# Query-weight casts moved from GpSimd to ScalarE, and a value copy moved ahead of the next unit's seed, in a two-layer linear-attention and gated-MLP kernel

## The chip, the cores and the metric

The kernel runs on one core of a Trainium2 chip. The metric is the device time of one execution in microseconds (us); the number given for a kernel is the median of several runs. One further execution is taken by the hardware profiler, and all rows of the profile come from it. The core's engines run side by side, each through its own instruction list in order: TensorE (PE in the profile, its weight loads PEld), VectorE (DVE), ScalarE (ACT), GpSimd (POOL), and SyncE (SP), which here issues the DMAs. [...]

## What is computed

Two kinds of blocks alternate, attention (A), MLP (B), A, B, each behind a layer norm and added to the running activations `x` (2048 x 1024, bf16). The changed code belongs to the second A.

```python
H = 32; Dh = D // H
qkv = (x @ wqkv) -> q, k, v per head
phi = lambda t: where(t > 0, t + 1, exp(t)) + 1e-6
pq, pk = phi(q), phi(k)
kv = einsum("bhsd,bhse->bhde", pk, v)      # summed over all tokens
z  = einsum("bhsd->bhd", pk)
num = einsum("bhqd,bhde->bhqe", pq, kv)
den = einsum("bhqd,bhd->bhq", pq, z)[..., None] + 1e-6
A   = (num / den) @ wo

B   = ((x @ w_gate) * (x @ w_up)) @ w_down

x = x + A(layernorm(x)); x = x + B(layernorm(x))    # twice
```

## The kernel before

**Stages.** Layers A, B, A, B follow one another in one program. Tokens are taken in 16 tiles of 128 and 4 groups of 512. The order of every engine's instructions is written out by hand: the program text, run once, appends each instruction to its engine's list, so what is written first runs first on that engine. Small plans (`at(step, f, ...)`) hang side work, such as layer norms, casts and loads, behind numbered steps of a stage's main loop.

**The stage of the change.** `kv_seven` makes keys and values of the second A layer. It computes each 2 x 2 block product with seven block products instead of eight, a Winograd form: sums of weight blocks (`w_sum`) and of activation blocks (`x_sum`) are made beforehand, and intermediate sums are taken out of PSUM between the products. The work comes in eight units (two per token group; each handles two token tiles). A unit has 14 steps, in the order of `SEQ`: `1k 5k 1v 6k 2k 6v 7k 5v 7v 4k 2v 3k 4v 3v`. The digit is the product, the letter says keys or values. Each step is four matmuls of 128x128 by 128x512 (L577) into one of five PSUM banks that the whole stage keeps: `ak`, `av` (products 1, 6, 7, 4), `ck`, `cv` (products 5, 3) and `b` (product 2, keys and values by turns).

Banks accumulate: 6k is added to what 1k left in `ak`, after that was read. So TensorE may begin a step only when earlier contents of its bank have been read. The readers of one unit, in the program's order:

- after 1k, ScalarE copies `ak` into `b`, the *seed* (L582), onto which 2k is then added;
- after 1v, 6v and 7v, ScalarE copies `av` to a temporary (L558); VectorE later adds `b` or `cv` to it and writes a value block (L561);
- after 6k and 7k, ScalarE copies `ak` into a 128x1024 scratch `wide` (L587); VectorE adds `ck` to its halves (L566), half 1 behind 7k and half 0 behind 3k;
- after 2k and 4k, ScalarE takes an exponential of the bank (L287, 128x512), and VectorE finishes phi (L291, L293) into the key scratch `pks`;
- after 3k, ScalarE takes the *wide* exponential over the 128x1024 scratch (also L287), and VectorE finishes it one step later;
- after 4v, ScalarE copies `av` to the last value block (`out4`, L569). `later(2, ...)` puts this two steps on: behind step 0 (1k) of the next unit, and there behind the seed.

The next unit's 1v (its step 2) overwrites `av`, so it needs that copy. After each unit but the first, 16 small matmuls (`kp`, L528) accumulate keys times values of the unit before.

**Side work in this stage.** Layer norms of the second half of the tokens: `ln_stats` on VectorE, then for some tiles `ln_norm` (two small ScalarE instructions, L258 and L260, then VectorE) and for the others `ln_rstd` (L242, L243) with `ln_apply` (L251, ScalarE, 128x1024), and then a DMA transpose (L274, SP). `x_sum` (L218) on VectorE. Loads and casts of the query weights: `load_w("q", 0)` and `load_w("q", 1)` behind steps 8 and 9 of unit 0 (1 MB each, SP's queue), then `cast_q` (L183) on GpSimd behind steps 20, 24, ... 48: eight casts of 128x1024 from bf16 to scaled f16, in place.

**Buffers.** `slots` is a first-in, first-out list of 17 scratch buffers; who calls `get()` first takes the one that was put back longest ago. `pks` and `wides` take theirs at the stage's start, before the query loads.

**Afterwards** `q_step` (L784) multiplies by the cast query weights: the first half (n = 0) for its steps 0 to 3, the second half for 4 to 7.

Of the kernel before, what the change touches and what calls it, by code (L numbers as in the profile page):

```python
# [9 lines left out]
ACT = mybir.ActivationFunctionType  # L10
ALU = mybir.AluOpType
# [24 lines left out]
def kernel(  # L36
# [11 lines left out]
    nc = tc.nc  # L48
# [4 lines left out]
    KD = D // P  # L53
# [5 lines left out]
    NB = 512  # L59
# [26 lines left out]
    def v3(s, n):  # L86
        return s[:].rearrange("p (k n) -> p k n", n=n)

    def h3(s, n):
        return s[:].bitcast(F16).rearrange("p (k n) -> p k n", n=n)  # L90
# [4 lines left out]
    def load_cols(view, n, parts=1):  # L95
        s = slots.get()
        w = KD // parts
        for r in range(parts):
            nc.sync.dma_start(out=v3(s, NB)[:, r * w:(r + 1) * w, :],
                              in_=view[:, r * w:(r + 1) * w, n * NB:(n + 1) * NB])  # L100
        return s
# [42 lines left out]
    for i in range(NV):  # L144
        vb = const.tile([P, KD, VW], BF16, tag=f"vb{i}", name=f"vb{i}")
# [10 lines left out]
    scw = const.tile([P, 6], F32, tag="scw", name="scw")  # L156
# [23 lines left out]

    def cast_q(n, i):
        s = wA["q"][n]
        nc.gpsimd.tensor_scalar(out=h3(s, NB)[:, 2 * i:2 * i + 2, :], in0=v3(s, NB)[:, 2 * i:2 * i + 2, :],  # L183
                                scalar1=scw[:, 4:5], scalar2=None, op0=ALU.mult)

    def w_blocks(which):
        a, b = (h3(s, NB) for s in wA[which])
# [19 lines left out]
    def x_blocks(g):  # L207
        x = h3(xnTs[(2, g)], NB)
        t = h3(xgs[g], 2 * P).rearrange("p (s k) n -> p s k n", k=KH)
        return x[:, 0:KH, 0:2 * P], x[:, KH:KD, 0:2 * P], x[:, 0:KH, 2 * P:NB], x[:, KH:KD, 2 * P:NB], t  # L210
# [73 lines left out]
    def phi_exp(b, c):  # L284
        m = temps.get()
        e = m[:].bitcast(BF16)[:, 0:b.shape[-1]]
        nc.scalar.activation(out=e, in_=b, func=ACT.Exp, bias=lns2[:, c:c + 1], scale=kaps[:, c:c + 1])  # L287
        return m, e
# [202 lines left out]
    def kv_seven(kvp):  # L491
        plan = {}

        def at(step, f, *args):
            plan.setdefault(step, []).append((f, args))

        for t, i in zip(range(2 * TPG, NT), (3, 8, 17, 31, 36, 45, 59, 64)):
            at(i, ln_stats, 2, t, (0,))
            if i % 14 == 8:
                at(i + 5, ln_norm, 2, t)  # L500
                at(i + 6, tr_tile, 2, t)
            else:
                at(i + 4, ln_rstd, 2, t)
                at(i + 6, ln_apply, 2, t)
                at(i + 7, tr_tile, 2, t)
        at(66, lambda: temps.put(st8.pop()))
        for g, i in ((1, 19), (2, 45), (3, 75)):
            for j in range(4):
                at(i + 2 * j, x_sum, g, j)
        at(8, load_w, "q", 0)  # L510
        at(9, load_w, "q", 1)
        for n in range(DC):
            for i in range(4):
                at(20 + 16 * n + 4 * i, cast_q, n, i)
        at(90, lambda: wA.update(o=[load_cols(wo_v, 0)]))

        pks = slots.get()
        pkv = v3(pks, D)
        SEQ = "1k 5k 1v 6k 2k 6v 7k 5v 7v 4k 2v 3k 4v 3v"
        bk = {key: banks.get() for key in ("ak", "av", "ck", "cv", "b")}  # L520
        wides = slots.get()
        wide = wides[:].bitcast(F32).rearrange("p (u n) -> p u n", n=D)

        def kp(t, first, last):
            u = t // TPG * 2 + t % 2
            r = 2 * (u % 2) + t % TPG // 2
            for c in range(KD):
                nc.tensor.matmul(out=kvp[c // 3][:, (c % 3) * VW:(c % 3) * VW + VW],  # L528
                                 lhsT=pkv[:, r, c * P:(c + 1) * P], rhs=vbs[r][:, c, :],
                                 start=first and c % 3 == 0, stop=last, skip_group_check=True)  # L530

        def tiles(u):
            return u // 2 * TPG + u % 2, u // 2 * TPG + u % 2 + 2

        def unit(u):
            g, pr = divmod(u, 2)
            b11, b21, b12, b22, t = x_blocks(g)
            lhs = {1: b11, 2: b21, 3: b22, 4: t[:, 3], 5: t[:, 0], 6: t[:, 1], 7: t[:, 2]}
            tm = {}
            r0 = 2 * (u % 2)  # L540

            def pk(i, n):
                return pkv[:, r0 + i, n * NB:(n + 1) * NB]

            def vb(i, n):
                return vbs[r0 + i][:, n * (NB // P):(n + 1) * (NB // P), 0:P]

            def w4(a):
                return a[:].rearrange("p (c f) -> p c f", f=P)

            wd2 = wide[:, u % 2]

            def later(n, f, *args):
                at(u * 14 + j + n, f, *args)

            def copy(key, b):
                tm[key] = temps.get()
                nc.scalar.copy(out=tm[key][:], in_=b[:])  # L558

            def add(out, key, b):  # L560
                nc.vector.tensor_tensor(out=out, in0=w4(tm[key]), in1=w4(b), op=ALU.add)  # L561
                temps.put(tm.pop(key))

            def addw(n, b):
                v = wd2[:, n * NB:(n + 1) * NB]
                nc.vector.tensor_tensor(out=v, in0=v, in1=b[:], op=ALU.add)  # L566

            def out4(b):
                nc.scalar.copy(out=vb(0, 1), in_=w4(b))  # L569

            for j, step in enumerate(SEQ.split()):
                i, w = int(step[0]), step[1]
                key = "b" if i == 2 else ("c" if i in (3, 5) else "a") + w
                b = bk[key]
                rhs = w_rhs(w, i)
                for k in range(KH):
                    nc.tensor.matmul(out=b[:], lhsT=lhs[i][:, k, pr * P:(pr + 1) * P], rhs=rhs[:, k, :],  # L577
                                     start=k == 0 and (i in (1, 5) or i == 2 and w == "v"), stop=k == KH - 1,
                                     skip_group_check=True)
                if i == 1:  # L580
                    if w == "k":
                        nc.scalar.copy(out=bk["b"][:], in_=b[:])  # L582
                    else:
                        copy("1v", b)
                elif i in (6, 7) and w == "k":
                    n = i - 6
                    nc.scalar.copy(out=wd2[:, n * NB:(n + 1) * NB], in_=b[:])  # L587
                    if i == 7:
                        later(1, addw, 1, bk["ck"])
                elif i == 6:  # L590
                    copy("6v", b)
                elif i == 7:
                    copy("7v", b)
                    add(vb(1, 1), "7v", bk["cv"])
                elif i == 3:
                    if w == "k":
                        addw(0, b)
                        later(1, phi_end, wd2, pkv[:, r0 + 1, :], 0, *phi_exp(wd2, 0))
                    else:
                        add(vb(1, 0), "6v", b)  # L600
                elif i == 2:
                    if w == "k":
                        phi_end(b[:], pk(0, 0), 0, *phi_exp(b[:], 0))
                    else:
                        add(vb(0, 0), "1v", b)
                elif i == 4:
                    if w == "k":
                        phi_end(b[:], pk(0, 1), 0, *phi_exp(b[:], 0))
                    else:
                        later(2, out4, b)  # L610
                for f, args in plan.pop(u * 14 + j, ()):
                    f(*args)

        for u in range(2 * NG):
            unit(u)
            if u > 0:
                for t in tiles(u - 1):
                    kp(t, u == 1 and t == 0, False)
            if u % 2 == 1:
                slots.put(xgs.pop(u // 2))  # L620

        for i in sorted(plan):
            for f, args in plan[i]:
                f(*args)
        slots.put(*wA.pop("k"), *wA.pop("v"), wS.pop("k"), wS.pop("v"), wS.pop("d"), wides)
        banks.put(*bk.values())
        wA["o"].append(load_cols(wo_v, 1))

        def rest():
            for t in tiles(2 * NG - 1):  # L630
                kp(t, False, t == NT - 1)
            slots.put(pks)
        return rest

    def load_w(which, n):
        wA.setdefault(which, []).append(load_cols(wqkv_v, {"q": 0, "k": DC, "v": 2 * DC}[which] + n))
# [645 lines left out]
```

## Time and profile before

| | us |
|---|---|
| runs of the kernel before (3) | 1502.18, 1501.54, 1501.65 |
| median | 1501.65 |
| the profiled execution's own time | 1502.76 |
| its span, first to last instruction | 1501.0 |
| units' matmuls (L577), from the first start to the last | 758.5 to 865.8 |
| busy in the window 800 to 814 (one unit): TensorE, VectorE, ScalarE | 13.70, 10.99, 8.79 |
| busy in the same window: GpSimd | 0.00 |
| the eight casts on GpSimd (L183), busy | 23.6 |

The rest of the span is layer B's products (L947, 3136 matmuls; L1187, 1568 matmuls) and the other parts of A. A row of the timeline reads: start, length, engine, line, operation, output and inputs, count of instructions merged into the row, and in brackets how long the engine was idle before it and what it had waited for. `b` is a PSUM bank, `s` a slot, `f` a temporary, `vb` a value block. Instructions of one engine overlap a little, so the next one's start can lie before the end of the one before. The mean granted TensorE clock of the profiled execution is 1.000 of full speed.

### The profile page before, as it was taken

The numbers are of one execution on the slowest core, as the hardware profiler recorded it, in microseconds if no ns is written. First come the engines' busy times: TensorE is split into PE (matmuls) and PEld (weight loads), VectorE is DVE, ScalarE is ACT, GpSimd is POOL, SyncE is SP. The second block draws the span as 40 slices with busy tenths as digits, with TensorE's granted clock in tenths as the row PEclk, the third lists the DMA queues.
The fourth block names the chain that finished last, engine by engine and source line by source line (L and its number), as shares of the span: only waits on it lengthen the run. The fifth ranks groups of instructions, "written<-read, shape, count | busy, mean of one in ns | idle before, by whom it ended". The sixth has DMA issues, their size and how long they took to land.

```text
span 1501.0 us, 18364 instructions
## 1 busy us (share of the span) xinstructions
PE 1488.1 (99%) x7075; PEld 683.3 (46%) x7109; DVE 988.4 (66%) x1659; ACT 803.9 (54%) x1177; POOL 114.1 (8%) x54
## 2 busy tenths in 40 slices
PE   9999999999999999999999999999999999999999
PEld 4454444444444444444444444444444444444444
DVE  6567989988676666667877586854445854444452
ACT  4678875776658477764546575623335223333420
POOL 0000004963000000000060000000000000000000
PEclk9999999999999999999999999999999999999999
DMA  8696136465479788759531101464333678343513
GB/s 245 172 304 232 57 92 202 132 208 153 130 211 313 250 263 263 246 200 267 164 84 23 42 29 28 132 235 168 121 125 109 188 261 325 113 168 113 209 61 130
DMA packets 219655, 253.90 MB, mean 169 GB/s; under 512 B 68528, under 2 KB 195504, under 8 KB 208816
## 3 DMA queue, kind: packets, MB, share of 16 engines
q1 hardware_dynamic: 219568, 252.74, 53.1%
q8 instruction: 55, 0.90, 0.2%
q14 instruction: 32, 0.26, 0.1%
HBM read 196.08 MB, written 40.89 MB: 158 GB/s over the span
## 4 chain that ended last, share of the span: by engine, by line
PE 96%; DVE 2%; ACT 1%; DMA 1%; issue 0%; SPq 0%; DVEq 0%; ACTq 0%
PE b L947 45%; PE b L1187 23%; PE b L784 7%; PE b L647 7%; PE b L815 7%; PE b L577 5%; PE b L798 1%; DMA s<-in_A_wqkv_dram 1%; PE b L666 1%; PE b L765 0%; PE b L528 0%; ACT b L582 0%; ACT vb L569 0%; DVE st L234 0%; DVE X L1160 0%
## 5 line engine op out<-in xcount | busy, mean ns | idle before, releaser
L947 PE MATMUL b<-s,s 128*128 128x512 f16 x3136 | 677.7, 379 | 0.0
L947 PEld LDWEIGHTS <-s 128*128 128x128 f16 x3136 | 306.8, 98 | 369.8
L1187 PE MATMUL b<-s,s 128*128 128x512 f16 x1568 | 339.1, 379 | 0.0
L963 DVE TENSOR_TENSOR f<-f,b 128x512 f32<-128x512 f32 x232 | 159.3, 687 | 223.7 <-ACT f L952 209.5
L952 ACT COPY f<-b 128x512 f32<-128x512 f32 x284 | 166.2, 585 | 224.8 <-PE b L947 224.8
L1187 PEld LDWEIGHTS <-s 128*128 128x128 f16 x1568 | 153.4, 98 | 185.0
L958 ACT COPY b<-b 128x512 f32<-128x512 f32 x104 | 59.3, 570 | 128.3 <-PE b L947 128.3
L444 ACT ACTIVATE s<-s,scw 128x1024 f16<-128x1024 bf16 x112 | 122.8, 1151 | 2.0 <-DMA s<-in_B_w_gate_dram 1.8
L784 PE MATMUL b<-s,s 128*128 128x512 bf16 (+1 forms) x508 | 119.9, 379 | 0.2
L815 PE MATMUL b<-s,s 128*128 128x512 bf16 x495 | 117.5, 379 | 1.1 <-DVE s L807 0.3
L913 ACT ACTIVATE s<-s,scw 128x1792 f16<-128x1792 bf16 x48 | 83.0, 1784 | 61.4 <-DMA s<-in_B_w_down_dram 61.4
L647 PE MATMUL b<-s,s 128*128 128x512 bf16 x500 | 111.3, 379 | 1.7 <-DMA s<-in_A_wqkv_dram 0.8
L868 POOL TENSOR_SCALAR s<-s,scw 128x1024 f16<-128x1024 bf16 x28 | 88.8, 3188 | 257.8 <-DVE X L817 244.1
L577 PE MATMUL b<-s,s 128*128 128x512 f16 x448 | 99.4, 379 | 3.6 <-ACT vb L569 3.5
L967 DVE SCALAR_TENSOR_TENSOR s<-f,b 128x512 f16<-128x512 f32 x108 | 74.2, 687 | 39.9 <-PE b L947 24.2
L967 DVE SCALAR_TENSOR_TENSOR s<-f,f 128x512 f16<-128x512 f32 x116 | 83.3, 718 | 4.5 <-DVE f L963 0.5
L815 PEld LDWEIGHTS <-s 128*128 128x128 bf16 x512 | 50.0, 98 | 60.9 <-DVE s L807 1.0
L647 PEld LDWEIGHTS <-s 128*128 128x128 bf16 x512 | 49.7, 98 | 60.7 <-issue 1.4
L784 PEld LDWEIGHTS <-s 128*128 128x128 bf16 (+1 forms) x512 | 50.0, 98 | 59.4
L234 DVE BATCH_NORM_STATS2 st<-X 128x6 f32<-128x512 bf16 x112 | 71.7, 681 | 2.6 <-DMA X<-in_A_x_dram 2.6
L577 PEld LDWEIGHTS <-s 128*128 128x128 f16 x448 | 43.5, 98 | 56.7 <-issue 6.4
L1095 DVE TENSOR_TENSOR s<-s,s 128x1024 f16<-128x1024 f16 x80 | 52.9, 678 | 23.4 <-PE b L1187 23.4
(123 smaller groups left out, 1113.2 us busy)
## 6 DMA issues: line engine op xcount, KB each, us to landing
s<-wc SPq DMA_DIRECT2D x56, 1024.0 KB, 6.6
s<-dc SPq DMA_DIRECT2D x32, 896.0 KB, 5.6
wc<-s SPq DMA_DIRECT2D x28, 1024.0 KB, 5.2
s<-in_B_w_down_dram SPq DMA_DIRECT2D x24, 896.0 KB, 5.6
s<-in_A_wqkv_dram SPq DMA_DIRECT2D x17, 1024.0 KB, 7.9
s<-in_B_w_down_dram SPq DMA_DIRECT2D x14, 1024.0 KB, 8.0
s<-in_B_w_gate_dram SPq DMA_DIRECT2D x28, 512.0 KB, 6.7
s<-in_B_w_up_dram SPq DMA_DIRECT2D x28, 512.0 KB, 7.7
```

Source lines behind the costliest of these rows:

```text
L444: nc.scalar.activation(out=h, in_=v, func=ACT.Copy, scale=scw[:, m:m + 1])
L577: nc.tensor.matmul(out=b[:], lhsT=lhs[i][:, k, pr * P:(pr + 1) * P], rhs=rhs[:, k, :], start=k == 0 and (i in (1, 5) or i == 2 and w == "v ...
L647: nc.tensor.matmul(out=b[:], lhsT=xnT[:, k, tl * P:(tl + 1) * P], rhs=w[:, k, :], start=(k == 0), stop=(k == KD - 1))
L784: nc.tensor.matmul(out=b[:], lhsT=w[:, k, j * P:(j + 1) * P], rhs=xnT[:, k, :], start=(k == 0), stop=(k == KD - 1))
L815: nc.tensor.matmul(out=b[:], lhsT=v3(pqs[g], G)[:, c, tl * P:(tl + 1) * P], rhs=v3(M[n], NB)[:, c, :], start=(c == 0), stop=(c == KD - 1))
L868: nc.gpsimd.tensor_scalar(out=h3(s, D)[:, i, :], in0=v3(s, D)[:, i, :], scalar1=scw[:, 2:3], scalar2=None, op0=ALU.mult)
L913: nc.scalar.activation(out=v.bitcast(F16)[:, r * w:(r + 1) * w], in_=v[:, r * w:(r + 1) * w], func=ACT.Copy, scale=scw[:, 2:3])
L947: nc.tensor.matmul(out=o[m][:], lhsT=W.get(j, m, st[i - 1], k), rhs=mv[i - 1][:, k, :], start=start and k == 0, stop=stop and k == KH - 1, ...
L952: nc.scalar.copy(out=d[m][:], in_=o[m][:])
L963: nc.vector.tensor_tensor(out=d[m][:], in0=d[m][:], in1=o[m][:], op=ALU.add)
L967: nc.vector.scalar_tensor_tensor(out=h3(hs[h], 2 * G)[:, pos, g * G:(g + 1) * G], in0=x[:], scalar=HS, in1=y[:], op0=ALU.mult, op1=ALU.mult)
L1187: nc.tensor.matmul(out=bank[(key, tl)][:], lhsT=lhs(i, j, tl), rhs=h3(wd[2 * pi + j // WPC], NB)[:, j % WPC, :], start=(j == 0 and i in (1 ...
```

## The change

Three edits in `kv_seven` and its helper. `cast_q` becomes a ScalarE activation (Copy with the same scale). The eight casts leave the plan: one is issued in each unit behind step 3k, ahead of the wide exponential, four for each half of the weights. The two loads of query weights leave the plan too and stand at the stage's head, before `pks` and `wides` take their slots. And `out4` is gone: the copy of the last value block is issued at step 4v itself.

```diff
     def cast_q(n, i):
         s = wA["q"][n]
-        nc.gpsimd.tensor_scalar(out=h3(s, NB)[:, 2 * i:2 * i + 2, :], in0=v3(s, NB)[:, 2 * i:2 * i + 2, :],
-                                scalar1=scw[:, 4:5], scalar2=None, op0=ALU.mult)
+        nc.scalar.activation(out=h3(s, NB)[:, 2 * i:2 * i + 2, :], in_=v3(s, NB)[:, 2 * i:2 * i + 2, :],
+                             func=ACT.Copy, scale=scw[:, 4:5])
...
-        at(8, load_w, "q", 0)
-        at(9, load_w, "q", 1)
         for n in range(DC):
-            for i in range(4):
-                at(20 + 16 * n + 4 * i, cast_q, n, i)
+            load_w("q", n)
         at(90, lambda: wA.update(o=[load_cols(wo_v, 0)]))
...
-            def out4(b):
-                nc.scalar.copy(out=vb(0, 1), in_=w4(b))
-
...
                 elif i == 3:
                     if w == "k":
                         addw(0, b)
+                        cast_q(*divmod(u, KD // 2))
                         later(1, phi_end, wd2, pkv[:, r0 + 1, :], 0, *phi_exp(wd2, 0))
...
                     if w == "k":
                         phi_end(b[:], pk(0, 1), 0, *phi_exp(b[:], 0))
                     else:
-                        later(2, out4, b)
+                        nc.scalar.copy(out=vb(0, 1), in_=w4(b))
```

## The prediction

> **What bounds the kernel now.** I read the page's busy line and chain of waits first, then the instructions of L577, the line that issues the changed stage's matmuls, and then the timeline over that stage.
>
> ```profile
> PE 1488.1 (99%) x7075; PEld 683.3 (46%) x7109; DVE 988.4 (66%) x1659; ACT 803.9 (54%) x1177; POOL 114.1 (8%) x54
> ...
> PE 96%; DVE 2%; ACT 1%; DMA 1%; issue 0%; SPq 0%; DVEq 0%; ACTq 0%
> ```
>
> TensorE is busy for 1488.1 of 1501.0 us, and 96% of the chain that ended last is its work. So only a hole in TensorE's stream can shorten the kernel. The instructions of L577 show who makes the holes of this stage:
>
> ```profile
> L577 PE MATMUL b<-s,s x448: 376/379/379, 758.5 to 865.8; 128*128 128x512 f16 x150
> its engine sat idle before it (us, times) until:
>   issue: 6.4, 10
>   ACT vb L569: 3.5, 7
> ```
>
> Seven times, once at each change from a unit to the next, TensorE waits for L569, ScalarE's copy of the value bank's last block. The "issue" row belongs to the weight loads: they idle between matmuls anyway. The timeline shows one change in full; this is unit 3 to unit 4 (units are counted from 0), and the other five late ones look alike:
>
> ```profile
> 801.70 10.52 PE L577 MATMUL b<-s,s 128*128 128x512 f16 x48 [0.30 <-ACT vb L569]
> ...
> 812.05 1.11 PE L528 MATMUL b<-vb,s 128*128 128x129 bf16 x16
> 812.58 1.24 ACT L287 ACTIVATE f<-s,lns,kaps 128x1024 bf16<-128x1024 f32 x1 [1.88 <-DVE s L566]
> ...
> 813.00 1.89 PE L577 MATMUL b<-s,s 128*128 128x512 f16 x8
> ...
> 814.06 0.57 ACT L582 COPY b<-b 128x512 f32<-128x512 f32 x1 [0.24 <-PE b L577]
> ...
> 814.54 0.59 ACT L569 CAST vb<-b 128x512 bf16<-128x512 f32 x1
> 815.19 10.52 PE L577 MATMUL b<-s,s 128*128 128x512 f16 x48 [0.30 <-ACT vb L569]
> ```
>
> ScalarE is free after the wide exponential, but its next instruction is the seed (L582), which needs the new unit's first product 1k; only behind that comes L569. TensorE does 1k and 5k (eight matmuls at 813.00), and then 1v must overwrite the bank that L569 still reads.
>
> The printed idle time is too small, because a matmul's modelled end (0.379 us) overlaps the next one's start. By starts: 48 matmuls run from 801.70 to 812.05, 10.35 us, 0.216 each. Eight from 813.00 would let the next start at 814.73; it starts at 815.19. **The hole is 0.46 us**, six times (restarts at 788.21, 801.70, 815.19, 828.68, 842.17 and 855.66, 13.49 apart): 2.78 us. The first change is worse:
>
> ```profile
> 768.95 1.10 DVE L291 TENSOR_SCALAR f<-f,scw,epss 128x512 bf16<-128x512 bf16 x1
> ...
> 771.28 0.68 DVE L566 TENSOR_TENSOR s<-s,b 128x512 f32<-128x512 f32 x1
> 772.00 1.24 ACT L287 ACTIVATE f<-s,lns,kaps 128x1024 bf16<-128x1024 f32 x1 [2.36 <-DVE s L566]
> 772.02 0.74 PEld L577 LDWEIGHTS <-s 128*128 128x128 f16 x4 [0.28 <-issue]
> ...
> 774.08 0.58 ACT L569 CAST vb<-b 128x512 bf16<-128x512 f32 x1
> 774.72 10.52 PE L577 MATMUL b<-s,s 128*128 128x512 f16 x48 [1.67 <-ACT vb L569]
> ```
>
> The 64 matmuls before it (timeline: 758.50, 14.54 us) end at 773.04 by the model, so the next could start 0.16 earlier (0.379 less 0.216), at 772.88. The hole to 774.72 is 1.84. Another 0.17 lies at 772.02: a weight load idles 0.12 in the steady stream (0.216 less its 0.098) and here 0.28. It starts 0.06 after L566 ended (771.96), which reads the bank that 5k overwrites. All holes together: 2.78 + 1.84 + 0.17 = 4.79 us.
>
> **The change, part by part.**
>
> *The value copy moves ahead of the seed.* No instruction is added; L569 now stands behind the wide exponential. At unit 3 to 4 the exponential starts at 812.58, and the next instruction on ScalarE can start 1.15 later (in another unit L258 starts at 799.98 after 798.83). The copy then runs 813.73 to 814.32, with its bank finished long before. 1v could start at 814.73: 0.35 to spare after the 0.06 of signalling (801.64 to 801.70 before). The other changes, likewise (exponential's start + 1.15 + 0.59 + 0.06 against 1k's start + 1.73): unit 1 to 2, 785.60 and 786.02, spare 0.35; 2 to 3, 798.83 and 799.50 (the restart at 801.70 less 0.46 and 1.73), spare 0.60; 4 to 5, 825.81 and 826.49, 0.61; 5 to 6, 839.57 and 839.98, 0.34; 6 to 7, 852.45 and 853.47, 0.95. All six holes close: 2.78.
>
> *The wait that this adds.* The seed now stands behind the copy. Late next would be 6k, which overwrites the bank that the seed reads, 0.86 (four matmuls) after 1v's start. At 3 to 4 the seed starts 0.48 behind the copy (the spacing of 814.06 and 814.54) and runs 814.21 to 814.78, 6k is due at 815.59. Tightest are units 2 and 4, where the norm's Ln and Exp (0.59 from L258's start to the seed's, 826.96 to 827.55) stand between copy and seed: at 4 to 5 the copy starts at 826.96, the Ln at 827.44, and the seed runs 828.03 to 828.60; 6k is due at 828.22 + 0.86 = 829.08, spare 0.4.
>
> *Eight casts on ScalarE.* The same form stands at L444, 128x1024 to f16 at 1.15 us, in the page. Eight make 9.2 us of ScalarE, each queued ahead of a wide exponential. They cost nothing if they fit ScalarE's idle time before that exponential, which waits for VectorE's L566: 2.36, 1.88, 1.61, 1.88, 1.61, 3.00, 2.40, 2.41 us for units 0 to 7 (timeline). In unit 0 this shrinks to about 1.67, by the next paragraph. All are above 1.15, the least spare 0.46. Without cover each would cost up to 1.15. Bounds of the cast: 1.13 (the shortest L444) and 1.23 (L251, as large, with two operands); I take 1.15, and nothing changes over that span.
>
> *Eight casts off GpSimd* (L183, 23.6 us from 760.32). Nobody waited for them. But in their time VectorE's L291 took 1.10 where the unit-3 row has 0.41, its wide form 1.46 against 0.55, and the wide L293 2.02 against 1.23. If the 0.69 at 768.95 is GpSimd's doing, L566 ends at 771.27 instead of 771.96. Then 5k's 0.17 closes, and the exponential starts at 771.31. The cast fits (L251 starts at 768.42, so the cast runs 769.55 to 770.70). The copy runs 772.46 to 773.05, and 1v starts at 773.11, where 772.72 was possible: gain 774.72 less 773.11, 1.61. If VectorE is no faster, the exponential stays at 772.00, the copy ends at 773.74 and 1v starts at 773.80: gain 0.92. I take 1.61: the three rows stretch only while GpSimd casts, though not always then (0.41 at 764.24). [...]
>
> *The query loads move to the stage's head.* They are two 1 MB transfers on SP's queue. The first transpose of the stage is issued behind step 10 of unit 0, they stood at steps 8 and 9, so they pass no other instruction of that queue. In the trace both are issued at 755.03 and used by 760.32; the median landing is 6.3 us. The first cast now wants its weights at 769.55. The loads take the two slots that the key scratch (pks) and the wide scratch had, and the other way round. Those scratches are first written at 762.56 (L587) and 764.68 (L293), after the last down-projection matmul (758.3). Cost nothing. The last cast ends near 864.7; the query matmuls begin at 866.96 with the other half of the weights.
>
> *Sum:* 2.78 + 1.61 = **4.4 us**, between 3.7 (0.92 at the first change) and 4.79 (every hole). The profiled execution took 1502.76 us, its span 1501.0 and 1.76 around it. That gives a span of 1496.6 and 1498.4 for such an execution. The median of the runs, 1501.65, lies 1.1 below the profiled one, so the forecast for it is 1497.3.
>
> **The rivals.**
>
> *The holes close by half.* The copy now depends on an exponential that waits for VectorE, with 0.35 us to spare in three changes; without holes, VectorE has 13.03 instead of 13.49 us for a unit. For it: VectorE is busy 11.0 of 14 us in the window from 800 to 814. Against: every unit shows VectorE idle before its wide exponential's result arrives (1.31 in most). If six holes keep 0.23 and the first gains 0.92: 2.3 us, 1499.3.
>
> *Saved here, waited for later.* If a later transfer or VectorE set the end, the 4.4 us would come back as a wait: 1501.6. Against: the next waits I see, 0.36 at 869.68 on VectorE and the output weights' second load (issued near 865.7, used at 877.5), follow TensorE's own progress and shift with it.
>
> *Slower: the query load blocks ScalarE.* GpSimd had nothing behind its casts; on ScalarE the first cast holds the exponential, the copy and the seed. The point is 770.15 (771.31 less 1.15): from there each microsecond of lateness stops TensorE as long. If the load were issued only with the transposes at 769.67 and took 7.9 (median landing of such loads over the kernel), the cast would run 777.6 to 778.7, the copy would end near 780.5, and 1v starts 5.8 later than before; less 2.8 for the six other holes that is 3.0 slower, 1504.6. Against: the load has a free queue and over 8 us of margin.
>
> **How the numbers follow.** Forecast 72%, half-closed 14%, no gain 8%, slower 6%. The likeliest gives 1497.3, its own range 1496.7 to 1498.0. To hold 8 in 10 I go to 1499.6, over the half-closed case, and down to 1496.6, all holes and 0.2 for the spread of the runs (0.6 us). A change of 0.2%, 3.0 us, is about what a measurement of this kernel can tell from none. The forecast lies beyond it, the half-closed case mostly within: faster 0.75, same 0.18, slower 0.07.
>
> **What would show it.** The profile after should have 1k, 5k and 1v in one stream at each change, so the group of L577 loses its 3.5 us behind the value copy; units 13.03 us apart; ScalarE in the order cast, wide exponential, copy, seed, with casts of 1.15 us; L291 at 0.41 in unit 0; no GpSimd work after the first down-projection casts; the query stage starting 4.4 us earlier. The prediction is wrong if the wide exponential starts later after 4k than now, if 6k waits for the seed, or if the first cast waits for a DMA.

## The result and the profile after

| | before | after |
|---|---|---|
| median of 13 runs, us | 1502.18 (1501.33 to 1502.66) | 1498.18 (1497.59 to 1499.31) |
| span of the profiled execution, us | 1501.0 | 1496.1 |
| units' matmuls, first to last start, us | 758.5 to 865.8: 107.3 | 758.0 to 860.9: 102.9 |
| GpSimd busy, us | 114.1 | 89.4 |
| ScalarE busy, us | 803.9 | 811.0 |

The changed kernel takes 0.9974 of the time before (95% interval 0.9966 to 0.9982): 4.0 us by the medians. The spans differ by 4.9, but 0.46 of that lies ahead of the stage, in code that is the same in both (its first matmul starts at 758.05 and before at 758.50). Over the ten traces of this case that start lies between 757.67 and 758.98, so it is a difference between executions. The stage itself is 4.4 us shorter.

The page's busy line and chain after:

```profile
PE 1489.2 (100%) x7109; PEld 683.0 (46%) x7109; DVE 985.5 (66%) x1659; ACT 811.0 (54%) x1185; POOL 89.4 (6%) x46
...
PE 97%; DVE 2%; DMA 1%; ACT 0%; SPq 0%; issue 0%; DVEq 0%; ACTq 0%
```

ScalarE's share of the chain, 1% before, is now printed as 0%. The units' matmuls are now issued by line L571:

```profile
L571 PE MATMUL b<-s,s x448: 376/379/380, 758.0 to 860.9; 128*128 128x512 f16 x150
its engine sat idle before it (us, times) until:
  issue: 1.2, 4
```

The seven waits for the value copy are gone; only the weight loads' "issue" row is left. It is worth reading: its four times are 0.27 and 0.37 in the first unit (at 759.06 and 761.04) and the 0.42 and 0.17 of the first change, shown below. The ten times of that row before were likewise the holes, as the weight loads see them: the timeline has 0.27 and 0.37 in the first unit, 0.28 and 1.95 at the first change and six of 0.58, together 6.4. The prediction took the row for an idling that is there anyway. The change from unit 3 to unit 4 in the timeline (L605 is the value copy, L576 the seed, L183 the cast, L525 the small matmuls):

```profile
806.46 1.23 ACT L251 ACTIVATE xn<-X,nmr,rstd 128x1024 f16<-128x1024 bf16 x1
...
807.59 1.14 ACT L183 ACTIVATE s<-s,scw 128x1024 f16<-128x1024 bf16 x1
...
809.03 1.11 PE L525 MATMUL b<-vb,s 128*128 128x129 bf16 x16
809.56 1.24 ACT L287 ACTIVATE f<-s,lns,kaps 128x1024 bf16<-128x1024 f32 x1 [0.83 <-DVE s L563]
...
809.97 5.34 PE L571 MATMUL b<-s,s 128*128 128x512 f16 x24
810.71 0.57 ACT L605 CAST vb<-b 128x512 bf16<-128x512 f32 x1
...
811.17 0.59 ACT L576 COPY b<-b 128x512 f32<-128x512 f32 x1
```

Read it against the same change before. The cast stands in what was ScalarE's idle time: 0.83 us are left of 1.88. The exponential still waits for VectorE (its bracket names L563, the later half of `wide`), so the cast did not move it: it starts 0.53 behind the small matmuls' first, as before (809.03 and 809.56; 812.05 and 812.58). The copy follows at once, the seed after it, and TensorE runs from 809.97 without a stop (24 matmuls in this view), where eight were followed by a hole. Over all eight units, the wide exponential's wait for VectorE fell from 17.1 to 8.1 us. That is 9.0, nearly what the casts now take (8 x 1.14 = 9.1).

The first change, in the timeline:

```profile
768.48 0.36 DVE L291 TENSOR_SCALAR f<-f,scw,epss 128x512 bf16<-128x512 bf16 x1
...
770.80 1.24 ACT L287 ACTIVATE f<-s,lns,kaps 128x1024 bf16<-128x1024 f32 x1 [0.57 <-DVE s L563]
771.95 0.56 ACT L605 CAST vb<-b 128x512 bf16<-128x512 f32 x1
...
772.56 0.74 PEld L571 LDWEIGHTS <-s 128*128 128x128 f16 x4 [0.42 <-issue]
...
773.48 9.16 PEld L571 LDWEIGHTS <-s 128*128 128x128 f16 x43 [0.17 <-issue]
```

VectorE's L291 is down from 1.10 to 0.36. The weight loads, idle 0.12 in the steady stream, show what is left: 0.30 before 1v (772.56) and 0.05 before 6k (773.48), which waits for the seed.

### The profile page after: what moved, and what is told of

Its sections match the earlier page's. It is cut to its first block, busy times and chain, and to the rows that moved or that the text cites. A ratio compares the mean times of both kernels' runs of the same rounds, so it can differ in the third digit from the quotient of the medians.

```text
span 1496.1 us, 18380 instructions
## 1 busy us (share of the span) xinstructions
PE 1489.2 (100%) x7109; PEld 683.0 (46%) x7109; DVE 985.5 (66%) x1659; ACT 811.0 (54%) x1185; POOL 89.4 (6%) x46
## 4 chain that ended last, share of the span: by engine, by line
PE 97%; DVE 2%; DMA 1%; ACT 0%; SPq 0%; issue 0%; DVEq 0%; ACTq 0%
PE b L942 45%; PE b L1182 23%; PE b L642 7%; PE b L779 7%; PE b L810 7%; PE b L571 6%; PE b L793 1%; DMA s<-in_A_wqkv_dram 1%; PE b L661 1%; PE b L760 0%; PE b L525 0%; DVE st L234 0%; DVE X L1155 0%; ACT f L287 0%; DVE X L812 0%; DVE s L293 0%
## 5 line engine op out<-in xcount | busy, mean ns | idle before, releaser
L571 PE MATMUL b<-s,s 128*128 128x512 f16 x448 | 98.3, 379 | 0.2
L571 PEld LDWEIGHTS <-s 128*128 128x128 f16 x448 | 43.5, 98 | 52.3 <-issue 1.2
```

## The experiments

Each kernel was run against the kernel before, whose medians in these two sets were 1502.57 and 1502.65. "Holes" are taken between the starts of single matmuls, less the steady 0.216 (0.06 for the small ones). "Stage" is from the first to the last start of the units' matmuls. Two small holes in the first unit (0.15 and 0.25) are in all ten traces alike and are left out.

| kernel | ratio to before (95%) | median, us | stage, us | hole at first change | holes at the six others |
|---|---|---|---|---|---|
| before | | 1502.2 to 1502.7 | 107.3 | 2.00 | 0.46 each |
| changed | 0.9974 (0.9966 to 0.9982) | 1498.18 | 102.9 | 0.36 | none |
| copy_only | 0.9976 (0.9966 to 0.9986) | 1498.98 | 103.8 | 1.24 | none |
| casts_only | 0.9996 (0.9988 to 1.0005) | 1502.11 | 106.6 | 1.26 | 0.46 each |
| cast_twice | 0.9973 (0.9962 to 0.9985) | 1498.88 | 103.4 | 0.85 | none |
| cast_thrice | 1.0014 (1.0005 to 1.0023) | 1504.82 | 108.8 | 2.03 | 1.04 to 1.10 in four |
| cast_behind_exp | 0.9998 (0.9989 to 1.0007) | 1502.50 | 106.9 | 1.40 | 0.66, 0.46, 0.66, 0.46, 0.67, 0.07 |
| gpsimd_late | 0.9972 (0.9961 to 0.9982) | 1498.41 | 102.9 | 0.36 | none |
| load_late | 1.0026 (1.0017 to 1.0035) | 1506.63 | 111.7 | 6.88 | none |
| both_orders | 0.9965 (0.9953 to 0.9978) | 1497.32 | 102.5 | none | none |

**One part alone: the copy.** Casts, loads and their places as before; only the value copy moves. The diff is against the kernel before.

```diff
-            def out4(b):
-                nc.scalar.copy(out=vb(0, 1), in_=w4(b))
...
-                        later(2, out4, b)
+                        nc.scalar.copy(out=vb(0, 1), in_=w4(b))
```

> The value copy moved, the query casts and loads as in the kernel before (GpSimd). Theory: the copy alone closes the six late holes (2.78 us) and takes 0.92 of the first; GpSimd still stretches VectorE in unit 0 (L291 about 1.1 us), so 0.17 stays before 5k and about 0.92 before 1v. 1502.2 less 3.7 = 1498.5. Rival: the casts' leaving GpSimd does nothing for the path; then the first change has the 0.36 of the changed kernel.

Its stage is 3.5 us shorter than before, and the six late holes are closed. The rest is the first change, where VectorE is still stretched:

```profile
760.62 17.11 POOL L183 TENSOR_SCALAR s<-s,scw 128x1024 f16<-128x1024 bf16 x6 [412.73 <-DMA s<-in_A_wqkv_dram]
...
769.11 1.23 DVE L291 TENSOR_SCALAR f<-f,scw,epss 128x512 bf16<-128x512 bf16 x1
...
772.29 1.24 ACT L287 ACTIVATE f<-s,lns,kaps 128x1024 bf16<-128x1024 f32 x1 [2.48 <-DVE s L566]
772.31 0.74 PEld L574 LDWEIGHTS <-s 128*128 128x128 f16 x4 [0.41 <-issue]
773.44 0.57 ACT L607 CAST vb<-b 128x512 bf16<-128x512 f32 x1
...
774.06 2.15 PE L574 MATMUL b<-s,s 128*128 128x512 f16 x9 [0.72 <-ACT vb L607]
```

This is the timeline of copy_only. With L291 at 1.23 the exponential starts at 772.29, behind an idle time of 2.48, and the copy ends too late for 1v: 0.89 by starts, with 0.30 before 5k at 772.31 and 0.05 before 6k. The stretching also leaves VectorE late inside unit 1, where a hole of 0.08 opens (781.95). So the copy brings most of the gain, as expected.

**The other part alone: casts and loads.** The changed kernel with the copy put back behind the next seed.

```diff
-                        nc.scalar.copy(out=vb(0, 1), in_=w4(b))
+                        later(2, lambda b=b: nc.scalar.copy(out=vb(0, 1), in_=w4(b)))
```

> Casts and loads as in the changed kernel, the value copy behind the next unit's seed as before. Theory: six holes of 0.46 stay; the first change shrinks from 2.01 to about 1.32, because VectorE is not stretched: 1501.5. Rival: the casts crowd ScalarE, and without the moved copy the kernel is slower than before, over 1502.2.

The six holes stay at 0.46, and the first shrinks from 2.00 to 1.26: the stage is 0.7 us shorter. The first change in the timeline of casts_only:

```profile
769.42 0.36 DVE L291 TENSOR_SCALAR f<-f,scw,epss 128x512 bf16<-128x512 bf16 x1
...
771.74 1.24 ACT L287 ACTIVATE f<-s,lns,kaps 128x1024 bf16<-128x1024 f32 x1 [0.57 <-DVE s L563]
...
774.45 0.81 PE L571 MATMUL b<-s,s 128*128 128x512 f16 x3 [1.10 <-ACT vb L605]
```

L291 is short here, and TensorE still waits for the copy. The whole kernel's 1502.11 cannot be told from the time before; the trace carries this verdict. The rival that casts crowd ScalarE fell.

**Was it GpSimd that stretched VectorE?** The copy moved, the casts on GpSimd again, but their loads late, so that they run in units 2 to 4. The diff is against the kernel before.

```diff
-        at(8, load_w, "q", 0)
-        at(9, load_w, "q", 1)
+        at(30, load_w, "q", 0)
+        at(31, load_w, "q", 1)
         for n in range(DC):
             for i in range(4):
-                at(20 + 16 * n + 4 * i, cast_q, n, i)
+                at(40 + 16 * n + 4 * i, cast_q, n, i)
...
-            def out4(b):
-                nc.scalar.copy(out=vb(0, 1), in_=w4(b))
...
-                        later(2, out4, b)
+                        nc.scalar.copy(out=vb(0, 1), in_=w4(b))
```

> The value copy moved; the query loads at steps 30 and 31 and the casts on GpSimd, which so run in units 3 to 5 and not in unit 0. Theory: what stretched VectorE in unit 0 was GpSimd's casting, so L291 there takes 0.36 to 0.41 and the first change has 0.36 as in the changed kernel, not the 1.18 of copy_only; stretched rows of VectorE appear in units 3 to 5, and an exponential that comes 0.7 later there passes the spare of 0.35, opening one or two holes up to 0.35: 0.9974 to 0.9979 of the kernel before. Rival: the start of the stage stretches VectorE by itself (transposes, the down projection's rest): then unit 0 keeps L291 at 1.1 and the first change its 1.18.

GpSimd casts from 789.4 to 812.2 here. VectorE's timeline of gpsimd_late, once before and three times within that time:

```profile
768.98 0.36 DVE L291 TENSOR_SCALAR f<-f,scw,epss 128x512 bf16<-128x512 bf16 x1
...
794.45 0.79 DVE L291 TENSOR_SCALAR f<-f,scw,epss 128x512 bf16<-128x512 bf16 x1
...
801.08 1.05 DVE L262 TENSOR_SCALAR xn<-X,mv,rstd 128x1024 f16<-128x1024 bf16 x1
...
807.18 0.58 DVE L291 TENSOR_SCALAR f<-f,scw,epss 128x512 bf16<-128x512 bf16 x1
```

The stretching went with the casts: unit 0's L291 is at 0.36, and rows that take 0.4 and 0.54 elsewhere are long while GpSimd casts, though not every one: the L291 at 803.49 keeps its 0.41. The loads do not stretch VectorE: in the changed kernel they are issued as early as before (754.65, before 755.03), and L291 takes 0.36. The first change has the 0.36 of the changed kernel. The one or two holes that were expected later did not open: L291's extra 0.4 in unit 2 and 0.2 in unit 3 stayed within the spare before 1v there (0.60 and 0.35). So the second part of the gain is not that ScalarE does the casts, but that GpSimd does not do them in unit 0. With the casts on GpSimd at a later time, the kernel is as fast.

**How much cover do the casts have?** One and two extra ScalarE passes of the same size over the same weights (a copy from bf16 to bf16, ahead of each cast, scaled by `ones`, a 128x1 tile set to 1.0 once at the start of the program).

```diff
     def cast_q(n, i):
         s = wA["q"][n]
+        for _ in range(1):     # range(2) in cast_thrice
+            nc.scalar.activation(out=v3(s, NB)[:, 2 * i:2 * i + 2, :], in_=v3(s, NB)[:, 2 * i:2 * i + 2, :],
+                                 func=ACT.Copy, scale=ones[:])
...
```

> A second ScalarE pass of the same size over the same weights ahead of each cast. Theory: the cast lies in ScalarE's idle time; of a second 1.04 us, 0.57 to 0.84 still lie in it, the rest (0.2 to 0.5) is under the spare of 0.35 to 0.6 before 1v, but not at the first change: loses about 0.6 on the changed kernel, 1498.8. Rival: ScalarE has no room, each extra pass costs its length: 8 x 1.04 = 8.3, 1506.5.

> Two extra passes. Theory: now the cover is gone: the exponential comes 1.2 to 1.5 us later in units 0 to 4, less the spare: holes of about 1.5 at the first change and 0.9 at the next four, 0.18 before 6k in units with a norm, 0.7 at the end: 6.3 lost, 1504.5, slower than before. Rival with room for any cast: 1498.8 again; rival with no room: 1498.2 + 16.6 = 1514.8.

The second pass costs 0.5 us in the stage, all of it at the first change; the third makes the kernel slower than before. It has holes at five changes and lengthens the wait for the last value sum behind the stage from 0.52 to 1.40. The same place in ScalarE's timeline of cast_twice and then of cast_thrice (L256 is the layer norm's pass, L186 is the extra pass, L188 the cast, L292 the exponential):

```profile
807.50 1.23 ACT L256 ACTIVATE xn<-X,nmr,rstd 128x1024 f16<-128x1024 bf16 x1
808.63 1.14 ACT L186 ACTIVATE s<-s,ones 128x1024 bf16<-128x1024 bf16 x1
809.80 1.15 ACT L188 ACTIVATE s<-s,scw 128x1024 f16<-128x1024 bf16 x1
810.85 1.22 ACT L292 ACTIVATE f<-s,lns,kaps 128x1024 bf16<-128x1024 f32 x1
```

```profile
810.42 1.23 ACT L256 ACTIVATE xn<-X,nmr,rstd 128x1024 f16<-128x1024 bf16 x1
811.55 2.32 ACT L186 ACTIVATE s<-s,ones 128x1024 bf16<-128x1024 bf16 x2
813.90 1.15 ACT L188 ACTIVATE s<-s,scw 128x1024 f16<-128x1024 bf16 x1
814.95 1.23 ACT L292 ACTIVATE f<-s,lns,kaps 128x1024 bf16<-128x1024 f32 x1
```

In both, the exponential's row has no bracket any more: it no longer waits for VectorE but follows the cast. Counted from the start of the layer norm's L256 (807.50 and 810.42), it starts 3.35 and 4.53 us later; in the changed kernel it is 3.10 (806.46 to 809.56). The second pass therefore pushes it by 0.25, under the spare of 0.35 before 1v. The third pushes it by 1.43; less 0.35 that is 1.08, and the trace shows a hole of 1.04. The first change had no spare left, so it pays from the second pass on.

**Does the cast's place matter?** The cast behind the exponential.

```diff
-                        cast_q(*divmod(u, KD // 2))
                         later(1, phi_end, wd2, pkv[:, r0 + 1, :], 0, *phi_exp(wd2, 0))
+                        cast_q(*divmod(u, KD // 2))
```

> The changed kernel with each cast behind the wide exponential instead of ahead of it, so between the exponential and the value copy. Theory: the cast has no cover there; the copy comes 1.04 us later, less the spare of 0.35 (units 1, 3, 5), 0.6 (2, 4) and 0.95 (6): holes of about 1.35 at the first change, then 0.69, 0.44, 0.69, 0.43, 0.70, 0.09: some 4 us lost on the changed kernel, so again about the time of the kernel before. Rival: where the cast stands does not matter, time as the changed kernel, 0.9974 of the kernel before.

The idle time before the exponential stays unused, and the cast stands in front of the copy. ScalarE and TensorE in the timeline of cast_behind_exp:

```profile
812.40 1.24 ACT L287 ACTIVATE f<-s,lns,kaps 128x1024 bf16<-128x1024 f32 x1 [1.87 <-DVE s L563]
...
813.55 1.14 ACT L183 ACTIVATE s<-s,scw 128x1024 f16<-128x1024 bf16 x1
...
814.59 0.57 ACT L605 CAST vb<-b 128x512 bf16<-128x512 f32 x1
...
815.21 5.12 PE L571 MATMUL b<-s,s 128*128 128x512 f16 x23 [0.50 <-ACT vb L605]
```

The same eight casts, one place further on, give nearly the whole gain back: 4.0 of 4.4 us in the stage. The expected holes (1.35, 0.69, 0.44, 0.69, 0.43, 0.70, 0.09) were met within 0.05.

**The slower rival made real.** The query loads behind step 10 of unit 0, so behind the first transpose of SP's queue.

```diff
         for n in range(DC):
-            load_w("q", n)
+            at(10, load_w, "q", n)
```

> The changed kernel with both query loads behind step 10 of unit 0, so behind the first transpose on SP's queue (issued near 769.5). Theory: the first cast waits for its weights until about 776 to 778 and holds the exponential, the copy and the seed behind it; TensorE stops before 1v of unit 1 for 5 to 7 us; the other holes stay closed: 1.0010 to 1.0025 of the kernel before. Rival: another wait or the queue's running ahead hides the load: 0.9974.

```profile
770.17 1.21 SPq L99 DMA_DIRECT2D s<-in_A_wqkv_dram  x2
775.95 1.15 ACT L183 ACTIVATE s<-s,scw 128x1024 f16<-128x1024 bf16 x1 [7.14 <-DMA s<-in_A_wqkv_dram]
777.00 1.23 ACT L287 ACTIVATE f<-s,lns,kaps 128x1024 bf16<-128x1024 f32 x1
778.13 0.57 ACT L605 CAST vb<-b 128x512 bf16<-128x512 f32 x1
...
778.75 7.46 PE L571 MATMUL b<-s,s 128*128 128x512 f16 x23 [6.71 <-ACT vb L605]
```

The timeline of load_late shows the chain of that rival step by step: load, cast, exponential, copy, 1v. The prediction priced 1v's delay against the kernel before at 5.8; here it is 4.9 (778.75 and 774.72, less the 0.84 by which this stage began earlier). Against the changed kernel, aligned in the same way, 1v comes 6.6 later and the stage is 8.9 longer; the other 2.3 are in the last section. The ratio, 1.0026, lies just above the 1.0010 to 1.0025 that was expected, because those 2.3 were not foreseen.

**A version below both.** The copy ahead of the wide exponential, and VectorE's sum behind 3v ahead of the wide phi's finish. Both follow from moving one line.

```diff
-                        later(1, phi_end, wd2, pkv[:, r0 + 1, :], 0, *phi_exp(wd2, 0))
...
                         nc.scalar.copy(out=vb(0, 1), in_=w4(b))
+                        later(1, phi_end, wd2, pkv[:, r0 + 1, :], 0, *phi_exp(wd2, 0))
```

> The changed kernel with two orders changed in each unit: the value copy ahead of the wide exponential on ScalarE, and VectorE's last value sum (behind 3v) ahead of the finish of the wide phi. Theory: ScalarE idles 0.57 or more before the exponential, the copy (0.57) fits there and no longer waits for VectorE; the first change closes (0.36), and the wait for the last value sum behind the stage (0.52) closes: 0.8 us below the changed kernel, 0.9968 of the kernel before. Rival: the copy pushes the exponential, or the finish of the wide phi is late for the next unit's VectorE work, and the holes come back elsewhere: 0.9974 or more.

All holes between units are gone, and so is the 0.52 behind the stage: in its trace the 16 small matmuls there run from 863.37 in one piece, where the changed kernel stops halfway for the last value sum (L558). The timeline of the changed kernel, then that of both_orders:

```profile
863.82 0.64 PE L525 MATMUL b<-vb,s 128*128 128x129 bf16 x8
...
864.81 0.63 PE L525 MATMUL b<-vb,s 128*128 128x129 bf16 x8 [0.36 <-DVE vb L558]
```

```profile
863.37 1.11 PE L525 MATMUL b<-vb,s 128*128 128x129 bf16 x16
```

By the traces that is 0.36 + 0.52 = 0.9 us. The median, 1497.32, is below both kernels, but the interval of its ratio (0.9953 to 0.9978) overlaps that of the changed kernel, so the times alone do not separate the two.

## Why the prediction was right

- *The late holes.* The step that took the hole by matmul starts (0.46) and not by the printed idle time (0.30) was needed: the stage got 4.4 us shorter, with all six closed, where all seven printed waits summed to 3.5. That the six are the copy's own is shown by copy_only, which closes them, and casts_only, which leaves them.
- *The first change.* Forecast 1.61 from two causes, measured 1.64 (2.00 to 0.36). copy_only and casts_only split it into 0.76 and 0.74 when each is made alone; together they bring a little more. The forecast's 0.92 for the copy alone was too high by 0.16, mostly since in that execution GpSimd stretched L291 to 1.23 and not to 1.10.
- *GpSimd's casts and VectorE's rows.* That the casts stretch rows of VectorE was argued from three rows; gpsimd_late shows it by moving the casts in time: L291 in unit 0 takes 0.36 there and 1.23 in copy_only. Why the rows stretch no run shows; not every row does (last section).
- *The loads' move.* It had next to no part in the gain. They were issued 3.4 us ahead of the stage's first matmul, before 3.5, and gpsimd_late, with the loads in unit 1 (783.48), has the same stage of 102.9.
- *The casts at nothing.* They cost nothing, in ScalarE's idle time, 0.57 us left where it is tightest. cast_twice and cast_thrice show where the cover ends: one more pass costs 0.5 us, and two lose more than the gain.
- *The added wait.* 6k waits for the seed only at the first change, 0.05 us. The prediction checked the other changes and missed that one. It had named a wait of 6k for the seed as a sign of being wrong; the sign came, but at a size that decides nothing.
- *The rivals.* "Closed by half" fell even with VectorE stretched (gpsimd_late). "Saved here, waited for later" fell: the 4.4 us stand at the end of the span, and the 0.52 behind the stage moved along unchanged. The slower rival did not occur, because the load had margin: issued from 754.65 with a median landing of 6.4 us, against a first cast at 769.09. Its mechanism is real (load_late), but its price was off in two places that partly cancel. The prediction said 3.0 us slower than before, and the medians give 4.0: the first cast started 5.8 us after the loads' issue where it had put 7.9, and the slow clock behind the stop (2.3 us, last section) was not in the sum.
- *The size.* The sum was 4.4; the stage gives 4.4, the medians 4.0. The median of 1498.18 is 0.9 above the forecast of 1497.3: the kernel before, with more runs, lies 0.5 higher than the 1501.65 it was set against, and the other 0.4 is within the spread of single runs (1497.59 to 1499.31). The 4.79 that the prediction called every hole leaves out the 0.15 and 0.25 in the first unit, which no version here closes.

## What to carry to other kernels

Where the critical engine waits for a copy, look at what stands before that copy in its engine's queue: here an instruction that needed the next unit's first product. In this kernel, work was added to an in-order engine without cost directly ahead of an instruction that waits for another engine. The bracket of that instruction is the room (1.88 us at the change shown, against casts of 1.14). One place further on, the same work cost its length less what spare there was behind it: 1.04 us at the first change, 0.07 to 0.67 at the others. Price a hole by the starts of the instructions around it, since modelled ends make it look smaller (0.46 by starts here, 0.30 as printed).

## What the runs showed of the hardware

After the 6.7 us stop of load_late, TensorE came back at half speed. The weight loads' rows there come 0.43 us apart instead of 0.216 (779.13, 779.56, 779.99, 780.41, and on to 783.40), and the stretches show the granted clock:

```profile
771.00:778.00 7.00, 1.04 (x5) 0.39 (x4) 0.00 (x0) 2.05 (x2) 0.00 (x0) 0.91 0.99 307
778.00:784.00 6.00, 5.25 (x14) 1.92 (x14) 3.64 (x6) 2.88 (x8) 0.00 (x0) 0.54 0.23 45
784.00:800.00 16.00, 16.00 (x88) 7.76 (x86) 11.83 (x22) 11.48 (x19) 0.00 (x0) 1.00 0.09 16
```

(Columns: the stretch, its length, busy time and count of TensorE, weight loads, VectorE, ScalarE and GpSimd, the granted clock, DMA share, GB/s.) The mean clock from 778 to 784 is 0.54 of full speed, and it is full again afterwards. If the clock stood at 1.00 or at 0.50 and nowhere between, 0.91 over the 7 us from 771 puts its fall near 776.7, and 0.54 over the 6 us from 778 its return near 783.5. By this estimate it fell some 4.7 us after the last matmul had ended (772.04) and came back some 4.8 us after the restart (778.75). By starts, twelve matmuls came 0.06 to 0.21 late, 2.3 us together, on top of the wait. In the nine other traces, whose longest hole between these matmuls is 2.03 us (cast_thrice), no weight load of theirs takes over 0.100 us; in load_late they take up to 0.147. What sets the two times no run shows: this is the only such stop. So the delay of that rival cost more than its length.

VectorE's L218, which takes both inputs from slots, kept its 0.67 to 0.73 while GpSimd cast (gpsimd_late, 802.89 to 809.1), where L291 took 0.58 (807.18, against 0.36 in unit 0) and L262 1.05 (801.08, against 0.54 at 774.89).
